# Values as bf16 in 1 KB reads, keys in 2 KB rows, early weights re-timed: an attention and spectral-mix kernel on one core

## Chip, cores, metric

The kernel runs on one core of a Trainium2 chip. The metric is device time in microseconds (us), the median of several executions; lower is better. All runs compared here are fast (within 1.5% of the fastest run of the same kernel).

## The reference

Sliding-window attention with a decay by distance, then a mix of the lowest 64 frequencies over the tokens by complex matrices, then a channel matrix. q, k, v are 8 x 8 x 576 x 64 in f32 (9.4 MB each); the spectral weights are 2 x 64 matrices of 512 x 512 in f32 (134 MB). One of them (the imaginary part of frequency 0) is not needed.

```python
scores = scale * q @ k.T                       # per batch and head, 576 tokens
scores = where(0 <= i - j < 128, scores - slope[h] * (i - j), -1e9)
x = concat_heads(softmax(scores) @ v)          # 8 x 576 x 512
X = rfft(x, axis=1)
Y[:, :64] = X[:, :64] * (w_r + 1j * w_i)       # per frequency a 512 x 512 matrix
u = x + irfft(Y)
out = u + relu(u @ w_ch)
```

## The kernel before

Attention comes first, in 16 units (8 batches x 2 groups of four heads). Work of neighbouring units is interleaved in "stages". The inputs of unit u + 2 are loaded when unit u's are cast to bf16. Meanwhile early spectral weights are fetched and converted to bf16 on the way (issued from GpSimd): one per stage, held back by a tiny "gate" copy that waits for an output of the stage before. After attention the other weights stream in as f32 into memory that attention leaves. Cuts are marked.

```python
# loads: values in pairs of tokens (j=2), so rows of 512 B; keys in nine tokens, rows of 2304 B
            t = self.raw[w][:, u % 2]
            sv = self.v[b, hs]
            for h in range(4):
                nc.sync.dma_start(
                    out=t[:, :2, h],
                    in_=sv[h, : FULL * P].rearrange("(r p j) d -> p r (j d)", r=2, j=2),
                )
            nc.sync.dma_start(
                out=t[64:96, 2],
                in_=sv[:, FULL * P :].rearrange("h (p j) d -> p h (j d)", j=2),
            )
        else:
            # ... queries and keys: one DMA of (j=9) rows

# cast of the values (VectorE)
        if w == "v":
            src = src.rearrange("p s h (j d) -> p s h j d", j=2)
            for half in range(2):
                row = slice(64 * half, 64 * half + 64)
                nc.vector.tensor_copy(
                    self.vb[u % 2][row, :, :, :, W * half : W * half + D], src[row, :2])
            nc.vector.tensor_copy(self.vt[u % 2][64:96, :, :, :D], src[64:96, 2])

# AHEAD: how many early weights at the end of which stage; EARLY: how many buffers they have; LATER: into the input buffers once they are free
    AHEAD = {0: 1, 1: 1, 2: 1, 4: 1, 5: 1, 7: 1, 8: 1, 10: 1, 11: 1, 12: 1, 13: 3, 14: 1}
    LATER = {14: 3, 15: 4}
    EARLY, NWA, NWB, AGAIN = 14, 6, 2, 8
# ...
            if stage in AHEAD:
                if stage:
                    b, g = at.units[stage - 1]
                    nc.gpsimd.tensor_copy(gate[:1, :1], x[:1, b, 0, 256 * g : 256 * g + 1])
                load_w(AHEAD[stage], early, True)
            if stage in LATER:
                load_w(LATER[stage], None, True)
# ... after attention: six f32 buffers in the memory it left
        load_w(NWA, wpool, False)
```

The softmax here doesn't subtract the row's maximum and nothing guards it: scores larger than these inputs give would overflow.

## Time and profile before

| | before |
|---|---|
| time, median of the first 4 runs | 451.56 us |
| DMA full | from about 3 to 411 us of the profiled 450.4 us |
| stage of attention (59 to 112 us) | 6.7 us |
| last early weight issued / first f32 weight issued | 124.4 / 125.9 us |
| first spectral matmul | 134.8 us |

In a table of stretches each row is one stretch of the span: its limits, its length, then the busy us of PE, PE weight loads, DVE, ACT and POOL (GpSimd), each with a count, then the granted clock, the DMA share (1 is all 16 engines busy; overlapping packets push it over 1) and GB/s. The prediction below shows that table. What it does not show are DVE's groups of instructions in steady attention, 59 to 112 us (line, engine, operation, out<-in, shapes, count | busy us, mean ns | idle us before):

```profile
L347 DVE TENSOR_TENSOR x<-av,rec 128x640 bf16<-128x640 f32 x16 | 13.2, 824 | 0.5
L233 DVE CAST vb<-vr 64x1024 bf16<-64x1024 f32 x16 | 10.9, 684 | 0.1
L305 DVE TENSOR_TENSOR att<-att,mask 128x1024 bf16<-128x1024 bf16 x16 | 10.3, 685 | 0.0
...
L235 DVE CAST vt<-vr 32x512 bf16<-32x512 f32 x8 | 3.3, 410 | 0.0
```

Eight units' values cost DVE 10.9 + 3.3 us of its 49.4, 1.8 us a unit.

### The profile page before, as it was taken

The numbers are of one execution on the slowest core, as the hardware profiler recorded it, in microseconds if no ns is written. First come the engines' busy times: TensorE is split into PE (matmuls) and PEld (weight loads), VectorE is DVE, ScalarE is ACT, GpSimd is POOL, SyncE is SP. The second block draws the span as 40 slices with busy tenths as digits, with TensorE's granted clock in tenths as the row PEclk, the third lists the DMA queues.
The fourth block names the chain that finished last, engine by engine and source line by source line (L and its number), as shares of the span: only waits on it lengthen the run. The fifth ranks groups of instructions, "written<-read, shape, count | busy, mean of one in ns | idle before, by whom it ended". The sixth has DMA issues, their size and how long they took to land. (4 is left out here: it accounts for less than half of the span.)

```text
span 450.4 us, 8021 instructions
## 1 busy us (share of the span) xinstructions
PE 362.3 (80%) x3314; PEld 193.1 (43%) x3314; DVE 177.0 (39%) x323; ACT 152.7 (34%) x196; POOL 73.9 (16%) x130
## 2 busy tenths in 40 slices
PE   4789899999968275776674766999999998877994
PEld 3457676777755032221222233544444443332331
DVE  7878699999752011010100132121212212220684
ACT  6859799999820000000000010211122110110772
POOL 8600000011512010200000000000000000054881
PEclk9989899999999659565659799999999999999998
DMA  8999999999999999999999999999999999995597
GB/s 282 310 310 319 302 232 303 321 311 263 212 266 319 316 260 314 326 372 427 418 421 421 423 422 419 420 421 420 421 418 421 421 420 421 420 399 206 197 358 295
DMA packets 53768, 157.03 MB, mean 349 GB/s; under 512 B 5205, under 2 KB 24421, under 8 KB 41317
## 3 DMA queue, kind: packets, MB, share of 16 engines
q1 hardware_dynamic: 47908, 140.56, 81.2%
q0 software_dynamic: 5824, 15.97, 18.1%
q8 instruction: 26, 0.43, 0.4%
q14 instruction: 10, 0.07, 0.0%
HBM read 162.53 MB, written 9.44 MB: 382 GB/s over the span
## 5 line engine op out<-in xcount | busy, mean ns | idle before, releaser
L832 PE MATMUL acc<-w,XC 128*32 128x512 bf16 x456 | 130.3, 451 | 42.5 <-DMA w<-in_moe_w_i_dram 22.1
L832 PEld LDWEIGHTS <-XC 128*32 128x32 bf16 x508 | 59.8, 139 | 127.5 <-issue 94.2
L294 ACT ACTIVATE att<-sc 128x1024 bf16<-128x1024 f32 x64 | 64.0, 1031 | 10.2 <-PE sc L284 10.2
L604 ACT CAST ZW<-zw 128x512 bf16<-128x512 f32 x8 | 4.7, 585 | 162.4 <-PE zw L602 162.4
L576 DVE TENSOR_SCALAR yq<-acc 128x512 bf16<-128x512 f32 x13 | 8.9, 688 | 104.6 <-PE acc L832 104.6
L679 ACT CAST XW<-my 128x512 bf16<-128x512 f32 x36 | 19.3, 589 | 75.4 <-PE my L627 75.4
L617 POOL DMA_DIRECT2D Z<-yq x19 | 9.7, 519 | 214.1 <-issue 207.7
L331 PE MATMUL av<-vb,att 128*128 128x132 bf16 (+1 forms) x576 | 39.0, 219 | 5.7 <-DVE x L347 3.9
L331 PEld LDWEIGHTS <-att 128*128 128x128 bf16 x704 | 37.2, 99 | 11.2 <-DVE x L347 8.2
L651 DVE COPY xT<-tr 128x1024 bf16<-128x1024 bf16 x18 | 12.5, 692 | 69.7 <-PE tr L649 69.7
L670 PE MATMUL my<-wch,xT 128*64 128x512 bf16 x288 | 34.5, 382 | 0.8 <-DVE xT L651 0.8
L256 ACT COPY qkT<-tp 128x1152 bf16<-128x1152 bf16 x30 | 33.5, 1116 | 3.2 <-PE tp L250 2.5
L284 PE MATMUL sc<-qkT 64*64 64x256 bf16 (+2 forms) x640 | 26.0, 271 | 2.1 <-ACT qkT L256 1.2
L347 DVE TENSOR_TENSOR x<-av,rec 128x640 bf16<-128x640 f32 x32 | 26.4, 824 | 1.1
L784 DVE TENSOR_TENSOR o<-yy,r 128x512 f32<-128x512 f32 (+1 forms) x24 | 21.7, 953 | 6.3 <-ACT r L741 4.6
L284 PEld LDWEIGHTS <-qkT 64*64 64x64 bf16 x640 | 15.0, 111 | 20.1 <-issue 17.1
L670 PEld LDWEIGHTS <-xT 128*64 128x64 bf16 x288 | 14.8, 109 | 18.9 <-issue 6.9
L271 PE MATMUL sc<-bias,ident 128*128 128x512 bf16 x64 | 21.4, 420 | 1.4 <-ACT att L294 1.4
L233 DVE CAST vb<-vr 64x1024 bf16<-64x1024 f32 x32 | 22.2, 694 | 0.3
L606 DVE CAST Z<-z 64x512 bf16<-64x512 f32 x16 | 11.0, 689 | 25.0 <-PE z L599 24.9
L741 ACT ACTIVATE r<-mm 128x512 f32<-128x512 f32 (+1 forms) x24 | 18.1, 811 | 7.4 <-PE mm L627 4.2
L305 DVE TENSOR_TENSOR att<-att,mask 128x1024 bf16<-128x1024 bf16 x32 | 20.6, 684 | 0.0
(133 smaller groups left out, 372.7 us busy)
## 6 DMA issues: line engine op xcount, KB each, us to landing
w<-in_moe_w_i_dram SPq DMA_DIRECT2D x52, 1024.0 KB, 18.0
w<-in_moe_w_r_dram SPq DMA_DIRECT2D x45, 1024.0 KB, 17.9
qr<-in_q_dram SPq DMA_DIRECT2D x16, 576.0 KB, 9.4
kr<-in_k_dram SPq DMA_DIRECT2D x16, 576.0 KB, 7.1
vr<-in_v_dram SPq DMA_DIRECT2D x64, 128.0 KB, 6.5
w<-in_moe_w_r_dram POOLq DMA_DIRECT2D x16, 512.0 KB, 17.3
out_dram<-o SPq DMA_DIRECT2D x10, 512.0 KB, 3.8
out_dram<-o SPq DMA_DIRECT2D x16, 256.0 KB, 3.5
```

The source lines that it names most:

```text
L233: nc.vector.tensor_copy(self.vb[u % 2][row, :, :, :, W * half : W * half + D], src[row, :2])
L256: (self.nc.vector.tensor_copy if u < 2 and w == "q" else self.nc.scalar.copy)(dst.rearrange("q h (p j) -> q h p j", j=TPP), tp.rearrange(" ...
L271: nc.tensor.matmul(sc[:, e], lhsT=self.ident, rhs=self.bias[:, hv].rearrange("p j n -> p (j n)"), start=True, stop=False, skip_group_check ...
L284: nc.tensor.matmul(sc[64 * half : 64 * half + 64, e, j * 256 + c0 : j * 256 + c0 + n], lhsT=qkT[row, 1, h, k0 + j : k0 + P : 2], rhs=qkT[r ...
L294: self.nc.scalar.activation(self.att[u % 2][:, kt * 8 * P : (kt + 1) * 8 * P], sc.rearrange("p e n -> p (e n)"), AF.Exp, scale=1.0 / math. ...
L305: nc.vector.tensor_tensor(out=rows, in0=rows, in1=self.table[:, heads], op=ALU.mult)
L331: nc.tensor.matmul(bank[:, qt * W : qt * W + rhs[j].shape[1]], lhsT=att[:, o : o + P], rhs=rhs[j], start=(n == 0 and j == 0), stop=(n == l ...
L347: nc.vector.tensor_tensor(out=self.x[:, b, :, cs].rearrange("p t (h d) -> p h t d", h=2), in0=tiles[:, :, :, :D], in1=rec.unsqueeze(-1).br ...
L670: nc.tensor.matmul(mm[ROWS[half]], lhsT=lhsT, rhs=wch[:, dt], start=(dt == 0), stop=False, skip_group_check=True,)
L679: nc.scalar.copy(XW[:, j, n], mms[n])
L784: nc.vector.tensor_tensor(out=o[:, c], in0=yy[:, c], in1=r[:, c], op=ALU.add)
L832: nc.tensor.matmul(into[32 * (i // 2) : 32 * (i // 2) + 32], lhsT=window[a], rhs=w[a], start=(ri == 0 and a == 0), stop=(ri == (m > 0) and ...
```

## The change

Its intent: read values in rows of 1 KB rather than 512 B, let the DMA convert them, and use the freed memory for one more early weight. Four tokens in a row land in one partition, so eight copies of 32 partitions bring the quarters to where the matmuls want them. Keys follow the same order of tokens. Buffers are laid out by parity of the unit so that slots for f32 weights come free earlier.

```diff
 def load:
         if w == "v":
-            for h in range(4):
-                nc.sync.dma_start(
-                    out=t[:, :2, h],
-                    in_=sv[h, : FULL * P].rearrange("(r p j) d -> p r (j d)", r=2, j=2),
-                )
+            nc.gpsimd.dma_start(                      # out is bf16
+                out=t[0],
+                in_=self.v[b, hs, : FULL * P].rearrange("h (p j) d -> p h (j d)", j=4),
+            )
+            # ... and the last 64 tokens with j=2
+        elif w == "k":
+            # ... rows of eight tokens (2 KB), the last 64 tokens in rows of two (512 B)
 def cast:
-            for half in range(2):
-                row = slice(64 * half, 64 * half + 64)
-                nc.vector.tensor_copy(
-                    self.vb[u % 2][row, :, :, :, W * half : W * half + D], src[row, :2])
+            for n in range(4):
+                c0 = W * (n % 2)
+                for a in range(2):
+                    r = 64 * (n % 2) + 32 * a
+                    nc.vector.tensor_copy(
+                        self.vb[u % 2][r : r + 32, n // 2, :, :, c0 : c0 + D],
+                        rows[32 * n : 32 * n + 32, :, :, a])
 # ... key transposes ten instead of nine, mask windows eight instead of four, layout by parity
-    AHEAD = {0: 1, 1: 1, 2: 1, 4: 1, 5: 1, 7: 1, 8: 1, 10: 1, 11: 1, 12: 1, 13: 3, 14: 1}
-    LATER = {14: 3, 15: 4}
-    EARLY, NWA, NWB, AGAIN = 14, 6, 2, 8
+    AHEAD = {0: 1, 1: 1, 2: 1, 3: 1, 4: 1, 5: 1, 7: 1, 8: 1, 9: 1, 10: 1, 11: 1, 12: 1, 13: 3}
+    LATER = {14: 3, 15: 2}
+    EARLY, NWA, NWB, AGAIN = 15, 6, 2, 8
 # ... start
-        for w, u in (("q", 0), ("k", 0), ("q", 1), ("k", 1), ("v", 0), ("v", 1)):
+        for w, u in (("q", 0), ("k", 0), ("q", 1), ("k", 1)):
             at.load(w, u)
 # ...
         at.distances(pool)
+        at.load("v", 0)
         at.fixtures(0)
         next(table, None)
+        at.load("v", 1)
         at.fixtures(1)
```

More of the change, by code (lines that the diff above doesn't have):

```diff
@@ L121, in __init__ @@
         fix = ctx.enter_context(tc.tile_pool(name="afix", bufs=1))
-        self.table = fix.tile([P, H, 2, 2 * P], BF16, name="mask")
-        self.bias = fix.tile([P, H, 2, 2 * P], BF16, name="bias")
-        self.vb = [fix.tile([P, 2, 4, 2, 2 * W], BF16, name=f"vb{i}") for i in range(2)]
-        self.vt = [fix.tile([P, 4, 2, W], BF16, name=f"vt{i}") for i in range(2)]
-        self.qkT = [fix.tile([P, 2, 2, (FULL + 1) * P], BF16, name=f"qkT{i}") for i in range(2)]
-        self.att = [fix.tile([P, FULL * 8 * P + 64], BF16, name=f"att{i}") for i in range(2)]
+        both = [[], []]
+        for i in range(2):
+            vb = fix.tile([P, 2, 4, 2, 2 * W], BF16, name=f"vb{i}")
+            vt = fix.tile([P, 4, 2, W], BF16, name=f"vt{i}")
+            att = fix.tile([P, FULL * 8 * P + 64], BF16, name=f"att{i}")
+            table = fix.tile([P, 4, 2, 2 * P], BF16, name=f"mask{i}")
+            bias = fix.tile([P, 4, 2, 2 * P], BF16, name=f"bias{i}")
+            qT = fix.tile([P, 2, S], BF16, name=f"qT{i}")
+            kT = fix.tile([P, 2 * S + 32], BF16, name=f"kT{i}")
+            both[i] = vb, vt, att, table, bias, qT, kT
+        self.vb, self.vt, self.att, self.table, self.bias, self.qT, self.kT = zip(*both)
         self.loaded, self.casted, self.open = {}, {}, {}
@@ L145, in distances, with window @@
         key_i = pool.tile([P, 2, 2], I32)
-        for half in range(2):
-            nc.gpsimd.iota(key_i[64 * half : 64 * half + 64], [[1, 2], [-P, 2]], base=0,
-                           channel_multiplier=2)
+        for r in range(4):
+            nc.gpsimd.iota(key_i[32 * r : 32 * r + 32], [[2, 2], [-P, 2]], base=r % 2,
+                           channel_multiplier=4)
+        last_i = pool.tile([P, 2], I32)
+        nc.gpsimd.iota(last_i[64:], [[1, 2]], base=0, channel_multiplier=2)
         key = pool.tile([P, 2, 2], FP32)
         nc.gpsimd.tensor_copy(key, key_i)
+        last = pool.tile([P, 2], FP32)
+        nc.gpsimd.tensor_copy(last[64:], last_i[64:])
         self.near = [pool.tile([P, 2, 2 * P], BF16) for _ in range(2)]
-        def window(out, half, c0, width, n):
-            row = slice(64 * half, 64 * half + 64)
+        def window(out, row, c0, width, n, values, first, j, p):
             sign = 1 - 2 * n
@@ L157, in window @@
                 out=out[row, :, c0 : c0 + width],
-                in_=key[row, :, n].unsqueeze(-1).broadcast_to([64, 2, width]),
-                compare_op=ALU.is_ge, fill=-float(2**20), base=-n,
-                pattern=[[-sign, 2], [sign, width]], channel_multiplier=-2 * sign,
-            )
-        for half in range(2):
+                in_=values.unsqueeze(-1).broadcast_to([row.stop - row.start, 2, width]),
+                compare_op=ALU.is_ge, fill=-float(2**20), base=-n - sign * first,
+                pattern=[[-sign * j, 2], [sign, width]], channel_multiplier=-sign * p,
+            )
+        for r in range(4):
+            row = slice(32 * r, 32 * r + 32)
             for n in range(2):
-                window(self.near[0], half, n * P, P, n)
+                window(self.near[0], row, n * P, P, n, key[row, :, n], r % 2, 2, 4)
         nc.gpsimd.tensor_copy(self.near[1][:64], self.near[0][:64])
         nc.gpsimd.tensor_copy(self.near[1][64:, :, : P + TAIL], self.near[0][64:, :, : P + TAIL])
-        window(self.near[1], 1, P + TAIL, TAIL, 0)
+        window(self.near[1], slice(64, P), P + TAIL, TAIL, 0, last[64:], 0, 1, 2)
     def slope(self, h):
-        return 2.0 ** (-8.0 * (h + 1) / self.table.shape[1])
+        return 2.0 ** (-8.0 * (h + 1) / (4 * self.NG))
     def decay(self, h):
-        self.nc.scalar.activation(self.table[:, h], self.near[0], AF.Exp, scale=self.slope(h))
+        self.nc.scalar.activation(self.table[h // 4][:, h % 4], self.near[0], AF.Exp, scale=self.slope(h))
     def offset(self, h):
-        self.nc.vector.tensor_scalar_mul(self.bias[:, h], self.near[1], math.sqrt(D) * self.slope(h))
+        self.nc.vector.tensor_scalar_mul(self.bias[h // 4][:, h % 4], self.near[1],
+                                         math.sqrt(D) * self.slope(h))
     def inverse_table(self):
@@ L204, in load @@
         if w == "v":
-            t = self.raw[w][:, u % 2]
-            sv = self.v[b, hs]
-            for h in range(4):
-                nc.sync.dma_start(
-                    out=t[:, :2, h],
-                    in_=sv[h, : FULL * P].rearrange("(r p j) d -> p r (j d)", r=2, j=2),
-                )
-            nc.sync.dma_start(
-                out=t[64:96, 2],
-                in_=sv[:, FULL * P :].rearrange("h (p j) d -> p h (j d)", j=2),
-            )
+            t = self.raw["v"][:, u % 2], self.raw["t"][64:96, u % 2]
+            nc.gpsimd.dma_start(
+                out=t[0],
+                in_=self.v[b, hs, : FULL * P].rearrange("h (p j) d -> p h (j d)", j=4),
+            )
+            nc.gpsimd.dma_start(
+                out=t[1],
+                in_=self.v[b, hs, FULL * P :].rearrange("h (p j) d -> p h (j d)", j=2),
+            )
+        elif w == "k":
+            t = self.raw[w][:, u % 2]
+            for e in range(2):
+                src = self.k[b, 4 * g + 2 * e : 4 * g + 2 * e + 2]
+                for row, j0, n, part in ((slice(0, P), 0, 8, src[:, : FULL * P]),
+                                         (slice(0, 64), 8, 2, src[:, FULL * P :])):
+                    nc.sync.dma_start(
+                        out=t[row, e, j0 : j0 + n].rearrange("p j d -> p (j d)"),
+                        in_=part.rearrange("h (p j) d -> p h (j d)", j=n),
+                    )
         else:
             t = self.raw[w][:, u % 2]
-            src = (self.q, self.k)["qk".index(w)][b, hs]
             nc.sync.dma_start(
                 out=t.rearrange("p e j d -> p e (j d)"),
-                in_=src.rearrange("(e h) (p j) d -> (h p) e (j d)", h=2, j=TPP),
+                in_=self.q[b, hs].rearrange("(e h) (p j) d -> (h p) e (j d)", h=2, j=TPP),
             )
@@ L229, in cast @@
         if w == "v":
-            src = src.rearrange("p s h (j d) -> p s h j d", j=2)
-            for half in range(2):
-                row = slice(64 * half, 64 * half + 64)
-                nc.vector.tensor_copy(
-                    self.vb[u % 2][row, :, :, :, W * half : W * half + D], src[row, :2])
-            nc.vector.tensor_copy(self.vt[u % 2][64:96, :, :, :D], src[64:96, 2])
+            rows = src[0].rearrange("p h (j a d) -> p h j a d", j=2, a=2)
+            for n in range(4):
[5 more added lines that the diff above has]
+                        rows[32 * n : 32 * n + 32, :, :, a])
+            nc.vector.tensor_copy(self.vt[u % 2][64:96, :, :, :D],
+                                  src[1].rearrange("p h (j d) -> p h j d", j=2))
         else:
-            dst = self.mid.tile([P, TPP, 2, D], BF16, tag=w, name=w)
+            dst = self.mid.tile([P, src.shape[2], 2, D], BF16, tag=w, name=w)
             nc.vector.tensor_copy(dst.rearrange("p j e d -> p e j d"), src)
@@ L244, in transpose @@
         src = self.casted.pop((u, w))
-        if (u, w) == (0, "k"):
-            tp = self.ps.tile([P, TPP, P], BF16, tag="sc", bufs=2, name="tp")
-        else:
-            tp = self.ps.tile([P, TPP, P], BF16, tag="tp", name="tp")
-        for j in range(TPP):
-            nc.tensor.transpose(tp[:, j], src[:, j].rearrange("p e d -> p (e d)"), self.ident)
-        self.open[w, u] = tp
+        tag = dict(tag="sc", bufs=2) if (u, w) == (0, "k") else dict(tag="tp")
+        tp = self.ps.tile([P, TPP * P], BF16, name="tp", **tag)
+        self.open[w, u] = tp
+        if w == "q":
+            for j in range(TPP):
+                nc.tensor.transpose(tp[:, j * P : (j + 1) * P],
+                                    src[:, j].rearrange("p e d -> p (e d)"), self.ident)
+            return
+        main = tp[:, : FULL * 2 * P].rearrange(
+            "d (h j b a i p) -> d j a i h b p", h=2, j=2, b=FULL, a=2, p=16, i=2)
+        rest = tp[:, FULL * 2 * P :].rearrange("d (j h i p) -> d j h i p", j=2, h=2, i=2)
+        for j in range(8):
+            nc.tensor.transpose(
+                main[:, j // 2 % 2, j % 2, j // 4], src[:, j].rearrange("p e d -> p (e d)"),
+                self.ident.rearrange("k (b p h) -> k h b p", b=FULL, h=2))
+        for j in range(2):
+            nc.tensor.transpose(
+                rest[:, j], src[:64, 8 + j].rearrange("p e d -> p (e d)"),
+                self.ident[:64, :64].rearrange("k (p i h) -> k h i p", i=2, h=2))
     def evacuate(self, u, w):
         tp = self.open.pop((w, u))
-        dst = self.qkT[u % 2][:, "qk".index(w), :, : self.S]
-        (self.nc.vector.tensor_copy if u < 2 and w == "q" else self.nc.scalar.copy)(
-            dst.rearrange("q h (p j) -> q h p j", j=TPP),
-            tp.rearrange("q j (h p) -> q h p j", h=2),
+        if w == "k":
+            self.nc.scalar.copy(
+                self.kT[u % 2][:, : 2 * self.S].rearrange("d (c p i) -> d c p i", p=16, i=2),
+                tp.rearrange("d (c i p) -> d c p i", p=16, i=2))
+            return
+        (self.nc.vector.tensor_copy if u < 2 else self.nc.scalar.copy)(
+            self.qT[u % 2].rearrange("q h (p j) -> q h p j", j=TPP),
+            tp.rearrange("q (j h p) -> q h p j", h=2, p=64),
         )
@@ L263, in score @@
         nc = self.nc
-        qkT = self.qkT[u % 2]
+        qT, kT = self.qT[u % 2], self.kT[u % 2]
         pair, h = t // 2, t % 2
@@ L269, in score @@
             for e in range(2):
-                hv = 4 * self.units[u][1] + 2 * e + h
                 nc.tensor.matmul(
-                    sc[:, e], lhsT=self.ident, rhs=self.bias[:, hv].rearrange("p j n -> p (j n)"),
+                    sc[:, e], lhsT=self.ident, rhs=self.bias[self.units[u][1]][:, 2 * e + h].rearrange("p j n -> p (j n)"),
                     start=True, stop=False, skip_group_check=True,
@@ L277, in score @@
                 blk = 2 * pair + half
-                spans = [(blk * P, 0, min(2 * P, self.S - blk * P))]
+                spans = [(512 * h + 256 * j + 64 * blk, blk * P, 0, min(2 * P, self.S - blk * P))]
                 if blk == FULL - 1:
-                    spans.append((FULL * P, 192, TAIL))
-                for k0, c0, n in spans:
+                    spans.append((FULL * 2 * P + 64 * j + 32 * h, FULL * P, 192, TAIL))
+                for k0, q0, c0, n in spans:
                     for e in range(2):
@@ L285, in score @@
                             sc[64 * half : 64 * half + 64, e, j * 256 + c0 : j * 256 + c0 + n],
-                            lhsT=qkT[row, 1, h, k0 + j : k0 + P : 2],
-                            rhs=qkT[row, 0, h, k0 : k0 + n],
+                            lhsT=kT[row, k0 : k0 + 64], rhs=qT[row, h, q0 : q0 + n],
                             start=not biased, stop=True, skip_group_check=biased,
@@ L303, in mask @@
         rows = att.rearrange("p (e j n) -> p e j n", e=2, j=2)
-        heads = slice(4 * g + t % 2, 4 * g + 4, 2)
-        nc.vector.tensor_tensor(out=rows, in0=rows, in1=self.table[:, heads], op=ALU.mult)
+        nc.vector.tensor_tensor(out=rows, in0=rows, in1=self.table[g][:, t % 2 :: 2], op=ALU.mult)
     def value(self, u, e):
@@ L433 @@
     rawpool = actx1.enter_context(tc.tile_pool(name="raw", bufs=1, side="right"))
-    raw = {w: rawpool.tile([P, 2, 2, TPP, D], FP32, name=w + "r") for w in "qk"}
-    raw["v"] = rawpool.tile([P, 2, 3, 4, 2 * D], FP32, name="vr")
+    raw = {w: rawpool.tile([P, 2, 2, n, D], FP32, name=w + "r") for w, n in (("q", TPP), ("k", 10))}
+    raw["v"] = rawpool.tile([P, 2, 4, 4 * D], BF16, name="vr")
+    raw["t"] = rawpool.tile([P, 2, 4, 2 * D], BF16, name="vtr")
     spare = [raw[w][:, i].rearrange("p e j d -> p (e j d)") for w in "qk" for i in range(2)]
-    vflat = raw["v"].rearrange("p u s h d -> p (u s h d)")
-    spare += [vflat[:, 2 * DM * i :] for i in range(3)]
-    spare = [t[:, : 2 * DM].bitcast(BF16).rearrange("p (a e) -> p a e", a=4) for t in spare]
+    spare = [t[:, : 2 * DM].bitcast(BF16) for t in spare]
+    spare.append(raw["v"].rearrange("p u h d -> p (u h d)"))
+    spare = [t.rearrange("p (a e) -> p a e", a=4) for t in spare]
     wq, homes, todo_w, again = {}, {}, [0, *range(2, 2 * NM)], []
@@ L462 @@
         n = len(at.units)
-        for w, u in (("q", 0), ("k", 0), ("q", 1), ("k", 1), ("v", 0), ("v", 1)):
+        for w, u in (("q", 0), ("k", 0), ("q", 1), ("k", 1)):
             at.load(w, u)
+        nc.vector.memset(raw["k"][64:, :, :, 8:], 0.0)
         done = set()
@@ L480 @@
         nc.vector.memset(norm[:32], 1.0 / S)
-        for t in at.qkT:
-            nc.vector.memset(t[:, 1, :, S:], 0.0)
+        for t in at.kT:
+            nc.vector.memset(t[:, 2 * S :], 0.0)
         at.distances(pool)
+        at.load("v", 0)
         at.fixtures(0)
         next(table, None)
+        at.load("v", 1)
         at.fixtures(1)
```

## The prediction

> **What bounds the kernel now.** I read the page's second part first (40 slices of the span), then the table of stretches, then the groups of instructions, then the DMA issues, then the packet records of the trace counted by size. From the page:
>
> ```profile
> PE   4789899999968275776674766999999998877994
> DVE  7878699999752011010100132121212212220684
> PEclk9989899999999659565659799999999999999998
> DMA  8999999999999999999999999999999999995597
> GB/s 282 310 310 319 302 232 303 321 311 263 212 266 319 316 260 314 326 372 427 418 421 421 423 422 419 420 421 420 421 418 421 421 420 421 420 399 206 197 358 295
> ```
>
> The DMA row is 9 from the second slice to the 36th (about 11 to 405 us), while no engine's row is. The GB/s row says that this full time buys about 420 GB/s in the second half but only some 300 in the first eleven slices, the attention. Part of that gap is only bookkeeping: the weights fetched early are converted from f32 to bf16 on the way, and the row counts the half-size written bytes. Counting source bytes from the packet records (twice the size for converting packets), I get 38.1 MB between 3 and 112 us, 349 GB/s, against 420 GB/s from 130 to 405 us. So attention loses about 109 x (1 - 349/420) = 18 us of DMA time. That is all a better load pattern can fight for. The table of stretches:
>
> ```profile
> 59.00:112.00 53.00, 50.01 (x920) 38.73 (x919) 49.38 (x90) 50.10 (x57) 5.95 (x12) 1.00 1.06 291
> 112.00:130.00 18.00, 15.92 (x293) 12.33 (x293) 12.69 (x25) 13.41 (x15) 7.13 (x13) 1.00 1.03 218
> 130.00:195.00 65.00, 40.53 (x214) 19.11 (x210) 8.71 (x27) 0.55 (x2) 8.89 (x20) 0.74 1.04 311
> 195.00:405.00 210.00, 174.09 (x977) 76.09 (x976) 35.97 (x73) 24.59 (x45) 6.34 (x13) 0.90 1.02 418
> ```
>
> After the stretch's length come busy us of PE, weight loads, DVE, ACT and POOL, then the granted clock, the DMA share and GB/s. In steady attention (59 to 112 us) PE, DVE and ACT are each 93 to 95% busy, so the three nearly tie, and the DMA share is 1.06 as well. From 130 us on only the DMA is full. The matmul group of the spectral stage waits for weights, and the queue's issues are deep:
>
> ```profile
> w<-in_moe_w_i_dram SPq DMA_DIRECT2D x52, 1024.0 KB, 18.0
> qr<-in_q_dram SPq DMA_DIRECT2D x16, 576.0 KB, 9.4
> kr<-in_k_dram SPq DMA_DIRECT2D x16, 576.0 KB, 7.1
> vr<-in_v_dram SPq DMA_DIRECT2D x64, 128.0 KB, 6.5
> ```
>
> A 1 MB weight needs 2.5 us at 420 GB/s and lands 18 us after issue: seven are queued. So until the last weight lands (about 411 us) the time is the sum of DMA work plus DMA idle time; the 39 us behind it (the chain that ended last starts at 416.6 us) are not touched. A faster or slower attention changes nothing by itself, as long as the DMA never runs dry.
>
> **The Trainium skill.** "DMA: Bandwidth & Descriptors", Specifications, puts the smallest transfer for line rate at 512 B. This trace differs: 512 B packets take 27 ns at the median (31 mean), 19 bytes per ns, where 8192 B packets take 313 (26 per ns). So there is something to gain in theory. The same page, "Issuing engines are not separate DMA queues", says all queues share the same 16 engines; the trace agrees (converting weights on the software queue take 0.69 of the engines between 130 and 160 us and the plain ones 0.35, sum 1.04), so moving values to another queue adds no rate. "SBUF - State Buffer", "SBUF: two separate sides", warns that descriptors written by GpSimd wait while DVE runs its two-port modes; here DVE is 93% busy, yet each of GpSimd's weight issues takes only 0.53 us. "VectorE: DVE Perf Modes", "What auto-detection actually checks": 16-bit copies inside SBUF can go twice as fast as f32 ones. The trace agrees: a 512-element bf16 copy takes 285 ns, a 512-element f32 cast 410.
>
> **The change part by part.**
>
> 1. Values, DMA. Removed: 18,432 packets of 512 B (16 units x 1152), mean 31.1 ns, over 16 engines 35.8 us. Added: 16 x 512 packets reading 1 KB and 16 x 128 reading 512 B, all converting. The trace has no such packet. A plain 1 KB packet takes 46 ns at its fastest; converting cost 322 against 313 ns at 8192 B and 96 against 84 at 2048 B (the late channel matrix against the output writes), so I add about 11: estimates 57 and 38 ns. Sum (8192 x 57 + 2048 x 38)/16 = 34 us unloaded, up to 39 us if load inflates it as it did the old ones (31.1/27). So **-2 to +3 us**: the bigger read is paid back by the conversion's fixed cost, since the number of packets only falls from 1152 to 640 and each costs nearly twice as much.
> 2. Keys, DMA. Was 4096 packets of 2304 B, mean 104.7: 26.8 us. Becomes 4096 of 2048 B (84 ns x the same 1.10 = 93) and 2048 of 512 B (31): 27.7 us. **+1 us**.
> 3. Weights. Early slots 14 to 15, two more early weights issued before stage 13 (at stages 3 and 9), late ones in spare buffers 7 to 5: 20 converted before the f32 stream instead of 21. The bytes from HBM are the same. One converting weight becomes plain: 128 x (331 - 316)/16 = 0.1 us. What it can gain is DMA idle time: the stretch from 55 to 60 us has a DMA share of 0.81, the only hole in attention, some 1 to 1.5 us. A weight at stage 3 (near 42 us) and faster refills should fill it: **-1 to -1.5 us**.
> 4. DVE. Per unit it drops 2 x 690 + 410 ns of value casts and gets eight 32-row bf16 copies of 512 elements and a tail, 9 x 0.28 = 2.5 us, +0.7 us; key cast +0.07 (1280 instead of 1152 elements). Overlap of neighbours (about 50 ns each) makes it +0.5. DVE had about 0.45 us of idle time in a 6.7 us stage, so DVE becomes the bound and the stage perhaps 7.0 to 7.2 us.
> 5. PE: ten key transposes for nine (about +0.1 us), contiguous 64-column score weights. ACT: same element counts, 1.12 us per evacuation.
> 6. Start: GpSimd makes eight distance windows instead of four (+2.5 us at 0.63 each) and issues the first values behind them, so the first exponentials come 1 to 2 us later. The queue then holds four 0.59 MB loads (some 6 us), so perhaps 0 to 1 us of DMA idle is added.
>
> Attention thus ends some 4 to 9 us later (it hands over at 134.8 us now), all beside a busy DMA. Inputs plus 20 weights are 28.3 + 21.0 = 49.3 MB, which at 349 GB/s from 3 us keep the DMA busy until 144 us. The reordered memory lets the first f32 slots open when the last even unit is done, before that. So I expect no hole at the handover.
>
> Sum: -2..+3, +1, -1.5, -0.1, 0..+1, centre about +0.5 us. I lean faster than that sum because mixed traffic inflates packets (2304 B: median 95, mean 104.7) and half as many value packets may lower this for queries and keys too: 8192 x 5/16 = 2.5 us. That gives about **450.5 us**.
>
> **Rivals.**
> (a) Bigger reads do remove most of attention's loss. For it: 512 B packets carry 13 of the 18 us of loss ((31.1 - 19.5) x 18,432/16). If a converting 1 KB packet cost only 46 ns loaded, values would take 27 us, 9 less, and with the hole the time would be about 442. Against it: the conversion surcharge.
> (b) DVE becomes the bound and the DMA runs dry at the handover. For it: the 93% and the added 0.5 us a stage, one weight fewer as buffer. Against it: the 10 us of queue above. It would cost 2 to 6 us: 454 to 458.
> (c) Values now stand behind whole weights in one software queue, and descriptors compete with DVE's ports; attention waits for values. For it: weights there land after 17.3 us. Against it: a value load has two stages, 13 us, and a weight ahead of it is 3 to 5 us. Lateness again counts only if the DMA idles; up to +5 us.
> (d) All of it is hidden, 452.
>
> **Range and chances.** 450.5, with (a) pulling to 443 and (b), (c) to 457: range 445 to 456. Faster by over 2% needs 9 us, all of (a): 0.07. Slower by over 2% needs 461, (b) and (c) together: 0.05. Within 2%: 0.88.
>
> **What would show it.** Value packets of 512 B written taking 50 to 65 ns (right) or 46 and less (rival a). DMA share near 1.05 with source rate near 350 GB/s in attention. DVE over 96% busy there, its eight copies at about 0.28 us; if they take 0.4, (b) gains. The first spectral matmul at 138 to 144 us while the DMA row stays 9; a digit below 9 near 130 to 145 us would be (b). The last weight landing 0 to 4 us earlier, with an unchanged tail. The prediction is wrong if the loss in attention came from mixing queues rather than from packet sizes, or if the tail moves.

## The result

The changed kernel takes 457.51 us (455.55 to 458.72, 4 runs) against 451.56 (450.14 to 452.37, 4 runs). The ratio is 1.0131, 95% interval 1.0086 to 1.0176. A ratio here is the mean time of one kernel's fast runs over the mean of the other's of the same rounds, so it is not quite the ratio of the medians quoted. The prediction, 450.5 with a range of 445 to 456, missed on the slow side.

The changed kernel's page, busy tenths in 40 slices of its 455.2 us:

```profile
PE   4578898889896755756766676999999999877993
DVE  6699899999983200010101024121212112220684
PEclk9999999999999977786566699999999999999999
DMA  8989999999899999999999999999999999996597
GB/s 266 203 216 279 274 257 241 245 275 271 125 201 285 316 314 318 326 380 425 421 421 421 422 423 418 421 419 420 422 420 420 420 419 421 420 402 243 194 354 293
```

DVE's digits stay at 8 and 9 two slices longer. The DMA row has an 8 in the third and in the eleventh slice (about 23 to 34 and 114 to 125 us), where it had a 9; GB/s in those slices are 216 and 125, where the kernel before had 310 and 212 (its slices are nearly as long). Part of that fall is bookkeeping, as the values, now converted, count half; the DMA shares below have no such effect. The table of stretches, on the changed kernel, with the same limits as in the prediction and finer ones below:

```profile
59.00:112.00 53.00, 47.67 (x838) 35.74 (x835) 51.22 (x125) 46.08 (x52) 18.53 (x26) 1.00 1.09 257
112.00:130.00 18.00, 16.54 (x287) 12.17 (x286) 16.82 (x41) 15.55 (x18) 8.87 (x14) 1.00 0.93 153
130.00:195.00 65.00, 43.54 (x350) 24.14 (x348) 15.13 (x44) 5.94 (x9) 9.45 (x21) 0.84 1.04 304
195.00:405.00 210.00, 176.11 (x974) 76.35 (x973) 36.66 (x74) 24.60 (x45) 3.89 (x8) 0.89 1.01 419
```

```profile
18.00:23.00 5.00, 0.40 (x12) 0.16 (x4) 4.87 (x8) 2.08 (x4) 4.40 (x8) 1.00 0.77 136
23.00:28.00 5.00, 2.81 (x32) 2.10 (x33) 4.94 (x13) 2.90 (x3) 2.46 (x3) 1.00 0.63 136
120.00:125.00 5.00, 4.71 (x85) 3.29 (x84) 4.49 (x10) 4.49 (x6) 4.38 (x8) 1.00 0.74 88
```

And the same stretches of five us of the kernel before:

```profile
18.00:23.00 5.00, 3.53 (x39) 2.82 (x40) 4.99 (x12) 4.58 (x6) 0.53 (x1) 1.00 1.04 272
23.00:28.00 5.00, 5.00 (x79) 3.51 (x80) 2.54 (x6) 2.96 (x3) 0.68 (x2) 1.00 1.06 353
120.00:125.00 5.00, 4.49 (x89) 3.63 (x86) 4.10 (x8) 3.98 (x6) 3.64 (x7) 1.00 1.06 213
```

The reader is to see two holes of the DMA, one near 18 to 28 us and one at 120 to 125 us, where the DMA share was above 1 before. DVE rose from 49.4 to 51.2 of 53 us, and its stage from 6.7 to 7.4 us (eight stages lie between the gate copies at 62.95 and 122.35 us). DVE's groups between 59 and 112 us in the changed kernel:

```profile
L252 DVE COPY vb<-vr 32x512 bf16<-32x512 bf16 x61 | 17.3, 284 | 0.7
...
L255 DVE COPY vt<-vtr 32x512 bf16<-32x512 bf16 x7 | 2.0, 285 | 0.2
```

The gate of stage 13, and the first weight of the burst behind it, in the kernel before and in the changed one:

```profile
112.48 0.51 POOL L524 COPY gate<-x 1x1 bf16<-1x1 bf16 x1 [5.67 <-DVE x L347]
112.94 0.53 POOL L451 DMA_DIRECT2D w<-in_moe_w_i_dram  x1
```

```profile
122.35 0.51 POOL L562 COPY gate<-x 1x1 bf16<-1x1 bf16 x1 [0.27 <-DVE x L381]
122.81 0.55 POOL L486 DMA_DIRECT2D w<-in_moe_w_i_dram  x1
```

**An account in bytes.** From the packet records I counted the source bytes landed by a given time (converting packets at twice their written size). In the streaming stage the DMA moves 0.42 MB per us, so a deficit divided by 0.42 is a lag in us. The third block is DMA idle time: the missing part of 16 packets in flight, summed.

| | landed by 30 us | 110 us | 125 us | 140 us | idle before 30 | 30 to 110 | 110 to 145 us |
|---|---|---|---|---|---|---|---|
| before | 9.8 MB | 37.5 | 43.1 | 49.4 | 2.4 us | 1.6 | 0.5 |
| changed | 7.5 | 37.0 | 41.2 | 47.2 | 7.0 | 1.8 | 2.9 |

The changed kernel is 5.3 us behind at 30 us (2.24 MB), catches up to 1.4 us at 110 us, falls back to 5.3 us at 140 us, and keeps that lag to the end of the weights: the last f32 weight packet ends at 415.9 us instead of 411.3. What follows then takes 39.3 us instead of 39.1. So the loss is made before 140 us, and the middle of attention looks **better** than before: 29.4 MB instead of 27.8 between 30 and 110 us.

### The profile page after: what moved, and what is told of

It is laid out like the page before. It is cut to its first block, busy times and chain, and to the rows that moved or that the text cites. A ratio compares the mean times of both kernels' runs of the same rounds, so it can differ in the third digit from the quotient of the medians.

```text
span 455.2 us, 8161 instructions
## 1 busy us (share of the span) xinstructions
PE 364.7 (80%) x3330; PEld 192.4 (42%) x3330; DVE 192.1 (42%) x420; ACT 152.9 (34%) x196; POOL 103.2 (23%) x170
## 5 line engine op out<-in xcount | busy, mean ns | idle before, releaser
L870 PE MATMUL acc<-w,XC 128*32 128x512 bf16 x464 | 134.7, 445 | 47.8 <-DMA w<-in_moe_w_r_dram 29.0
L252 DVE COPY vb<-vr 32x512 bf16<-32x512 bf16 x128 | 39.0, 305 | 3.7 <-DMA vr<-in_v_dram 2.2
L216 POOL DMA_DIRECT2D vr<-in_v_dram x16 | 18.2, 1140 | 59.4 <-DVE vb L252 59.4
L320 PE MATMUL sc<-qT,kT 64*64 64x256 bf16 (+2 forms) x640 | 25.5, 267 | 2.6 <-ACT kT L289 2.0
L320 PEld LDWEIGHTS <-kT 64*64 64x64 bf16 x640 | 14.7, 110 | 19.6 <-issue 16.0
```

Of the source, the lines that this page charges most:

```text
L216: nc.gpsimd.dma_start(out=t[0], in_=self.v[b, hs, : FULL * P].rearrange("h (p j) d -> p h (j d)", j=4),)
L252: nc.vector.tensor_copy(self.vb[u % 2][r : r + 32, n // 2, :, :, c0 : c0 + D], rows[32 * n : 32 * n + 32, :, :, a])
L320: nc.tensor.matmul(sc[64 * half : 64 * half + 64, e, j * 256 + c0 : j * 256 + c0 + n], lhsT=kT[row, k0 : k0 + 64], rhs=qT[row, h, q0 : q0 ...
L870: nc.tensor.matmul(into[32 * (i // 2) : 32 * (i // 2) + 32], lhsT=window[a], rhs=w[a], start=(ri == 0 and a == 0), stop=(ri == (m > 0) and ...
```

## The experiments

Theory H: the time is lost in holes, in which nothing is issued to the DMA. Loads and early weights are issued stage by stage, and the stage got longer through DVE. Rivals: P, the new packets cost more DMA time; S, the late start alone is to blame. Kernels ran beside the kernel before, whose median was 451.73 us (e1 to e4), 449.57 (e5 to e8), 450.31 (e9 to e11) and 449.58 (e12; one run of the kernel before took 1591 us, that the ratios leave out). Compare ratios, not times. The trace of the kernel before that is used throughout is not of these: e6 is level with it by the ratio (1.0002), yet its profiled span is 2.0 us shorter (448.4 against 450.4). So the leads over that trace given for e8, e10 and e12 may be about 2 us too large.

| run | median us | ratio to before | 95% interval |
|---|---|---|---|
| changed | 457.51 | 1.0131 | 1.0086 to 1.0176 |
| e1_start | 457.64 | 1.0132 | 1.0106 to 1.0159 |
| e2_burst | 452.88 | 1.0036 | 1.0009 to 1.0064 |
| e3_start_burst | 454.32 | 1.0067 | 1.0038 to 1.0096 |
| e4_half_copies (wrong result) | 450.89 | 0.9987 | 0.9959 to 1.0016 |
| e5_before_dve | 455.58 | 1.0129 | 1.0093 to 1.0165 |
| e6_spread | 449.86 | 1.0002 | 0.9973 to 1.0031 |
| e7_before_vpool | 455.52 | 1.0134 | 1.0100 to 1.0168 |
| e8_pool_copies | 448.77 | 0.9978 | 0.9952 to 1.0005 |
| e9_cast512 | 448.32 | 0.9944 | 0.9913 to 0.9975 |
| e10_start_pool4 | 451.27 | 1.0001 | 0.9970 to 1.0032 |
| e11_start_pool2 | 450.90 | 1.0001 | 0.9969 to 1.0032 |
| e12_before_spread | 454.18 | 1.0090 | 1.0042 to 1.0138 |

### e1_start: fill the first hole

```diff
         at.load("v", 1)
+        load_w(2, early, True)
         at.fixtures(1)
-    AHEAD = {0: 1, 1: 1, 2: 1, ...
+    AHEAD = {2: 1, ...
```

> The changed kernel, with its first two early weights issued right after the values of unit 1 (near 17 us) instead of at the ends of stages 0 and 1 (24.8 and 32.6 us); nothing else moves. Theory H (holes: the DMA has nothing issued from 18 to 28 us and again from 120 to 125 us): the first hole closes (DMA share 18 to 28 us from 0.77 and 0.63 to about 1), but the number of early weights before the last burst at the end of stage 13 is the same, so what is gained at the start is lost again as a longer second hole near 120 us. Time 457 +-1.5. Rival P (the converting packets and the 512 B key tails simply cost more engine time, 38.1 against 35.8 us and 28.7 against 26.8 us by their records): also about 457, but with no hole near 120 us longer than before. Rival S (the start hole alone cost the 5 us): 452 to 453.

Measured: 457.64 us, nothing gained. The first hole did close (DMA share 1.08 and 1.04 from 18 to 28 us, lag at 30 us down to 0.8 us). From 120 to 125 us the share was 0.73, and the lag at 125 us 4.3 us (4.6 in the changed kernel). Rival S falls: by 115 us the lags behind the kernel before were 0.6 us (changed) and 0.3 (e1): both kernels had worked off nearly all that was issued, and a better start was waited away. Between 30 and 110 us e1 landed 27.8 MB, no more than the kernel before.

### e2_burst: fill the second hole

```diff
-    ... 11: 1, 12: 1, 13: 3}
+    ... 11: 1, 12: 4}
```

> The changed kernel with the three weights of the end of stage 13 issued at the end of stage 12 (near 115 us instead of 123 us); nothing else moves. Theory H: the second hole (DMA share 0.74 from 120 to 125 us) closes and 3 to 4.5 us come back: 453 to 454.5. Rival P: no hole matters, 457. Rival S: 457.

Measured: 452.88 us, by the ratios some 4.3 us less than the changed kernel. The second hole is gone:

```profile
120.00:125.00 5.00, 4.89 (x88) 3.81 (x88) 4.50 (x11) 4.49 (x5) 3.26 (x6) 1.00 1.06 211
```

The packets are the same, so P does not explain the loss. Nearly three quarters of it was this one hole: queries and keys were all loaded at about 116 us, only the last unit's values (0.6 MB of f32) were still to be issued, at 120.4 us, and the last burst of weights stood behind the gate of stage 13 until 122.8 us (112.9 us before the change).

### e3_start_burst: both

The edit is that of the two runs above together.

> Both moves of weights together. Theory H: both holes are filled, and as source bytes flow somewhat faster in the middle of attention than in the kernel before (368 against 346 GB/s between 30 and 115 us), the kernel comes out 7 to 9 us faster than the changed one: 448.5 to 451, at or just under the kernel before (451.6). Rival P: 457. Rival S: 452 to 453.

Measured: 454.32 us, a miss of theory H by 3 us or more. Its lag at 30 us was 0.9 us, yet 0.5 at 115 us and 1.6 at 140 us. What the start gains is still lost between 30 and 110 us, where DMA idle time and slack come with one weight a stage or none. A hole can only be turned into time if later stages issue more as well.

### e4_half_copies: less DVE work (wrong result)

```diff
-                for a in range(2):
+                for a in range(2 if u < 2 else 1):
```

> Wrong result on purpose: from unit 2 on, four of the eight quarter copies of the values are left out, 4 x 0.28 = 1.1 us of DVE less a unit, DMA and its schedule untouched. Theory H with DVE as the cause of the second hole: stage length falls from 7.4 to about 6.7 us, the last burst comes near 113 us, the attention ends 8 to 10 us earlier, the second hole closes and 3 to 4 us come back: 453 to 454; the start hole stays. Rival P: 457, as attention's length does not matter to a full DMA.

Measured: 450.89 us, better than expected, and level with the kernel before, though neither the loads nor the schedule were touched. The stage fell to 7.0 us, the last burst came at 116.6 us, and between 30 and 110 us 30.2 MB landed. So DVE's copies are a cause: they pace every issue, not only the end of attention.

### e5_before_dve: the same DVE burden on the kernel before

```diff
             nc.vector.tensor_copy(self.vt[u % 2][64:96, :, :, :D], src[64:96, 2])
+            for _ in range(3):
+                nc.vector.tensor_copy(self.idle[:32, 1], self.idle[:32, 0])   # 32 x 512 bf16, unused
```

> The kernel before with three idle 32-row bf16 copies of 512 elements (0.28 us each) added to DVE after each unit's value casts, loads and schedule untouched. Theory H2 (a longer DVE stage alone makes the DMA run dry, because loads and early weights are issued stage by stage): stage from 6.7 to about 7.4 us, the last bursts of weights come 8 to 10 us later, a DMA hole appears between about 112 and 125 us, time 454.5 to 457. Rival D (attention's length is hidden behind a full DMA, as the prediction had it): 451.5 to 452.5, DMA share 1.0 throughout.

Measured: 455.58 us, ratio 1.0129, as large as the whole loss of the change (the two need not add up: the change also has its start hole on one side and its cheaper inputs on the other). The copies took 282 ns, the stage became 7.2 us, and a hole opened some ten us before the place of the second one of the changed kernel (the last burst came at 116.3 us here):

```profile
110.00:115.00 5.00, 4.12 (x79) 3.51 (x79) 4.78 (x13) 4.32 (x6) 0.00 (x0) 1.00 0.80 157
115.00:120.00 5.00, 4.61 (x85) 3.59 (x82) 4.61 (x9) 4.70 (x6) 2.04 (x4) 1.00 0.83 161
```

Rival D of that run, and with it the prediction's main premise, falls: 0.85 us more DVE work per unit (3 x 282 ns; the change adds 2.56 - 1.79 = 0.77) is not hidden behind the DMA.

### e6_spread: the same weights, issued evenly and earlier

```diff
-    AHEAD = {0: 1, 1: 1, 2: 1, 3: 1, 4: 1, 5: 1, 7: 1, 8: 1, 9: 1, 10: 1, 11: 1, 12: 1, 13: 3}
+    AHEAD = {0: 1, 1: 1, 2: 1, 3: 1, 4: 1, 5: 1, 6: 1, 7: 1, 8: 1, 9: 1, 10: 1, 11: 2, 12: 2}
```

> The changed kernel with the same fifteen early weights issued by the end of stage 12, but spread: one also at stage 6, two at stages 11 and 12, none at 13. Theory H: the DMA is starved of issues wherever a stage has no weight; against the version with three moved to stage 12 (452.9) the hole near 75 us and the slack of the middle are filled too: 450.5 to 452. Rival P or no slack left in the middle: 452.5 to 454, and values landing later behind weights.

Measured: 449.86 us, ratio 1.0002: the schedule alone takes back the whole loss, with DVE as busy as in the changed kernel (51.2 of 53 us). DMA idle time falls to 0.5 us between 30 and 110 us and to 0.1 from there to 145 us:

```profile
59.00:112.00 53.00, 46.51 (x832) 35.45 (x838) 51.19 (x125) 45.88 (x52) 20.29 (x30) 1.00 1.12 264
120.00:125.00 5.00, 4.89 (x87) 3.81 (x87) 4.50 (x11) 4.49 (x5) 3.30 (x6) 1.00 1.18 206
```

### e7_before_vpool: values on the other queue, unconverted

```diff
-                nc.sync.dma_start(out=t[:, :2, h], ...      # values of the kernel before, f32
+                nc.gpsimd.dma_start(out=t[:, :2, h], ...
```

> The kernel before with the values still as f32 in 512 B packets but issued from GpSimd, so on the other queue, as in the changed kernel. It tells why the busy DMA moved 368 GB/s of source bytes between 30 and 115 us in the changed kernel against 346 before. If two queues overlapping each other's packets is the reason: some 365 GB/s here while busy too (mean packets in flight above 18). If the larger reads are: about 346. Time itself is not the point (GpSimd has ten issues a stage; later start): 451 to 457.

This run asks why the middle looks better. I took the busy DMA time between 30 and 110 us (16 packets in flight counting as full), subtracted 2.5 us per MB-sized weight (at the streaming rate), and divided by the MB of inputs: 3.02 us per MB in the kernel before, 2.80 in the changed one, 2.77 in e6, and about 3.0 here. So moving the values to the other queue alone did not make inputs cheaper. But the packets did not stay the same, as was intended: the 18,432 value packets of 512 B became 2304 records of 4096 B (178 ns at the median).

The count also moves with the schedule. With the loads of the changed kernel it is 2.93 in e1 and 2.94 in e3, where 8.0 weights landed in the stretch, against 2.77 in e6 and 2.74 in e8 with 10.3 and 10.7. With the loads of the kernel before it is 3.04 in e5 with 8.0 and 2.90 in e12 with 10.9. So about half of the fall from 3.02 goes with the number of weights, and the loads are only to be compared at a like number. The time (455.52) is no answer by itself: with the values issued from GpSimd the DMA share was 0.88 from 18 to 23 us and 0.73 from 115 to 120 us.

### e8_pool_copies: half of the copies on GpSimd (right result)

```diff
-                    nc.vector.tensor_copy(
+                    (nc.gpsimd if u > 1 and a else nc.vector).tensor_copy(
 # with the AHEAD of e6_spread
```

> The spread weights of the other run of this call, and from unit 2 on four of the eight quarter copies on GpSimd instead of DVE (right result). GpSimd is 35% busy in attention and a 64-row copy took it 0.6 us, so 4 x 0.6 = 2.4 us fit in its stage. Theory H: DVE falls by 1.1 us a unit as in the run with half the copies (450.9, stage 6.9 us), the second hole is closed by the schedule as well, so 448 to 450. Rival: GpSimd and DVE block each other and DVE's instructions get longer, stage stays near 7.4 us: 452.

Measured: 448.77 us, ratio 0.9978; the interval just touches 1. The rival had a part in it, for the copies that stayed on DVE took longer:

```profile
L252 DVE COPY vb<-vr 32x512 bf16<-32x512 bf16 x30 | 13.5, 452 | 0.3
```

452 ns instead of 284, so of the 1.1 us a unit that left DVE some 0.7 came back (4 x 0.17), and the stage was 7.1 us.

### e9_cast512: conversion without the larger reads

```diff
-    raw["v"] = rawpool.tile([P, 2, 3, 4, 2 * D], FP32, name="vr")
+    raw["v"] = rawpool.tile([P, 2, 3, 4, 2 * D], BF16, name="vr")
-                nc.sync.dma_start(out=t[:, :2, h], ...      # 512 B rows as in the kernel before
+                nc.gpsimd.dma_start(out=t[:, :2, h], ...
 # layout, keys, masks and the two 64-row casts as in the kernel before;
 # EARLY 15 and AHEAD as in e6_spread, LATER {14: 3, 15: 2}, start of the values as in the change
```

> The kernel before with its values still read in 512 B pieces (two tokens) but converted to bf16 on the way from GpSimd, keys as before, no quarter copies: three DVE copies of bf16 a unit (two of 64 rows x 1024, about 0.4 us each, and the tail 0.28 = 1.1 us, against 1.79 before and 2.6 in the changed kernel). Freed memory goes to a fifteenth early slot, early weights in the spread schedule. It parts the two halves of 'bf16 in 1 KB reads'. Counting weights at 2.5 us each, the busy DMA spent 3.02 us per MB of inputs between 30 and 110 us in the kernel before, 2.99 with the values on GpSimd's queue unconverted, 2.75 to 2.81 with the change. If the 1 KB reads are what helps: 3.0 or more here (pieces written are only 256 B). If the conversion helps by itself: about 2.8. Time: DVE at 6.2 us a stage, so no longer stage than before; 447 to 452, the better the cheaper the conversion.

Measured: 448.32 us, ratio 0.9944 (0.9913 to 0.9975), the only version clearly under the kernel before. Inputs cost 2.83 us per MB. At a like number of weights that stands between 2.90 (e12, neither conversion nor larger rows) and 2.77 and 2.74 (e6 and e8, both); over the stretch from 40 to 110 us the same four are 2.80, 2.90, 2.80 and 2.75. So conversion without 1 KB reads brings a part of the gain, from not quite half to all of it; the count is too coarse to say more. And without quarter copies DVE is relieved instead of loaded:

```profile
59.00:112.00 53.00, 48.12 (x865) 37.31 (x865) 41.51 (x83) 46.66 (x52) 31.37 (x50) 0.97 1.22 264
112.00:130.00 18.00, 16.92 (x301) 12.96 (x302) 13.09 (x27) 16.10 (x20) 9.37 (x16) 1.00 1.20 202
```

DVE is busy 41.5 of 53 us (49.4 before, 51.2 changed), and the DMA has no idle time after 40 us. The value casts are now 64x1024 bf16 copies of 422 ns (684 from f32).

### e10_start_pool4 and e11_start_pool2: all repairs together

The edits are those of e1, e6 and e8; e11 puts two of the eight copies on GpSimd (`a and n > 1`) instead of four.

> The changed kernel with all three repairs: two early weights at the start, the rest spread to stage 12, and four of eight quarter copies on GpSimd from unit 2 on. Theory H: with the middle of attention full, the 2.5 to 3.5 us that the start hole costs are no longer lost later, so 1 to 2.5 us faster than without the start weights (0.9978 of before): ratio 0.992 to 0.997. Rival: values and queries of the first units come later behind the two weights and attention shifts: 0.998 to 1.0.

> As the run with all three repairs, but only two quarter copies on GpSimd. With four there, the copies left on DVE took 452 ns instead of 284[...]. If that blocking grows with the number on GpSimd, two save DVE about as much (0.5 us a unit) as four, and the ratio is within 0.002 of the other.

Measured: 1.0001 both. e10 misses its expectation, and its own rival's figure fits. In its profile the start did pay up to 120 us (5.4 us ahead of the kernel before, 4.5 in e8), but everything issued was done by then, and the weights into the input buffers were not issued before 122.5 us: the DMA share was 0.88 from 120 to 125 us (in e8 they came at 123.0, and the share was 0.95). Its profiled execution (span 447.0) does not show why the timed runs were slower than e8's by 0.2%; that stays open. e11 has the same ratio as e10, as expected: with two copies on GpSimd those on DVE took 293 ns, with four 470, so DVE was spared about 0.5 us a unit by two and 0.4 by four. That this is why the times are equal is not shown.

### e12_before_spread: the even schedule on the kernel before

```diff
-    AHEAD = {0: 1, 1: 1, 2: 1, 4: 1, 5: 1, 7: 1, 8: 1, 10: 1, 11: 1, 12: 1, 13: 3, 14: 1}
+    AHEAD = {0: 1, 1: 1, 2: 1, 3: 1, 4: 1, 5: 1, 6: 1, 7: 1, 8: 1, 9: 1, 10: 1, 11: 1, 12: 2}
```

> The kernel before, with only its fourteen early weights moved forward to one per stage and two at stage 12, as in the repaired kernels. It tells how much of the 0.9944 of the 512 B converting version is the schedule. If the schedule alone does it: 0.993 to 0.996. If the DMA of the kernel before has no slack to fill (busy share 0.98 between 30 and 110 us, 2 us of idle), at most 0.5 us: 0.998 to 1.0, and weights earlier only make inputs land later.

Measured: 454.18 us, ratio 1.0090, worse than either expectation. So e9's gain is not the schedule alone. The trace shows the opposite failure: the bytes landed ran 3.7 us ahead by 110 us, the inputs came late (DVE waited 7.9 us for queries and 5.1 us for values between 20 and 130 us; in the kernel before 2.4 us for queries, and values are not among the waits listed), attention ended later, the first f32 weight was issued at 140.1 us instead of 125.9, and the DMA, all early slots filled, ran dry:

```profile
130.00:135.00 5.00, 4.31 (x62) 3.71 (x63) 2.70 (x5) 1.70 (x2) 0.00 (x0) 0.66 0.99 227
135.00:140.00 5.00, 3.87 (x74) 2.92 (x72) 3.88 (x7) 3.04 (x5) 1.05 (x2) 1.00 0.16 20
```

I read it so: with inputs at 2.8 us per MB (e6) such a schedule fits, and with the dearer inputs of the kernel before (2.90 in this run) it does not. No run varies that cost alone, so this is not shown. Nor does any run part the conversion in e9 from the DVE time that it saves.

## Why the prediction was wrong, point by point

- **What bounds the kernel.** "A faster or slower attention changes nothing by itself, as long as the DMA never runs dry" was true as worded, and the step that failed is the next one, "So I expect no hole at the handover" (from "keep the DMA busy until 144 us"). I divided all prefetchable bytes by a rate and forgot that bytes count only once they are issued. Weights are issued by stage number; a longer stage moved the last burst from 113 to 123 us, while all queries and keys had landed by 116 us. So the DMA share was 0.74 from 120 to 125 us (1.06 before), and 2.9 us of DMA time stood idle from 110 to 145 us (0.5 before). e5 shows that the stage alone costs 1.29%, e2 and e6 that issuing earlier gives most (1.0036) or all (1.0002) of it back.
- **Rival (b)** named this outcome (454 to 458) and came true; I weighed it too lightly. Its site was only nearly right: the hole lay before the last burst, not after it.
- **Part 4, DVE:** the copies took 284 ns as said; the stage became 7.4 us, not 7.0 to 7.2, and DVE 96.6% busy. The first spectral matmul came at 144.3 us, 9.5 us later ("4 to 9"). Right in kind, somewhat small. The agreement claimed with the VectorE page is one of direction: 410 to 285 ns is a factor of 1.44, not two.
- **Part 6, start:** "perhaps 0 to 1 us of DMA idle" was 4.5 us (7.0 against 2.4 before 30 us). The first values were issued at 10.0 us, their first eight copies took 5.0 us instead of 2.4 beside GpSimd's fills, and the next query cast stood behind them. Other executions of the same start had 5.0 to 5.8 us (e2, e4). Yet e1 shows that this hole costs nothing as long as later stages have slack.
- **Part 1, packets of values:** 60 ns (64 mean) and 41 ns; "50 to 65" held, and the sum of records is 38.1 us, inside my "34 to 39". But as DMA time it was misleading: the records sum to more than before (35.8 us), yet more packets are in flight at once (17.8 against 16.9 between 30 and 110 us), and the inputs became cheaper by 0.22 us per MB; at a like number of weights it is 0.10 to 0.16, over the 28.3 MB some 3 to 4.5 us if it held throughout. So a part of the gain sought by rival (a) exists; e9 shows that some of it comes with the conversion alone. The added "lean" of 2.5 us for less inflation was in the right direction. Taken whole it would have given 449.6 (451.6 + 0.5 - 2.5); the 450.5 takes only some 1.6 of it, and does not say why.
- **Part 2, keys:** 2048 B rows and 512 B tails could not be told apart from the rest. No run isolates them.
- **Part 3, weights:** two more before stage 13 and none at 14 did not fill the holes, as the extra ones came at stages 3 and 9.
- **Rival (c):** values landed 7.8 us after issue, well within two stages; no wait of DVE for them beyond 2.2 us at the start. It did not happen.
- **The tail** stayed: 39.3 against 39.1 us.
- **A reading:** 0.69 and 0.35 of the engines for the two queues are, on the clock of the views, of 119.5 to 149.5 us. From 130 to 160 us I count 0.53 and 0.50; the sum is 1.04 in both.

## What to carry to other kernels

A full DMA hides compute only where transfers are already issued: if issues are tied to stages of compute, a longer stage shifts every later issue, so work out when each transfer is issued, not only how many bytes are left. Do not add up packet durations as DMA time when packets overlap; compare bytes landed by time. Judge a load pattern by what it makes the busiest engine do afterwards: the plain conversion (e9) brought a part of the DMA gain and took work off DVE (41.5 of 53 us), where the 1 KB rows brought eight copies a unit (51.2). And before two loads are compared by a rate, see what the rate does when only the schedule moves.

## What the Trainium skill lacked or had wrong

- "DMA: Bandwidth & Descriptors", Specifications, gives 512 B as enough for line rate: here 512 B packets took 27 ns at the median (19 bytes per ns, against 26 at 8192 B), and inputs made of 2304 and 512 B packets cost 3.02 us per MB where large weights cost about 2.4 (1/0.42). That the size of the packets alone is the reason is not shown: in e7 the values' records were of 4096 B, and the cost was still about 3.0.
- The same page has no figure for what conversion costs: records of converting packets were 41 ns (256 B written), 60 (512), 96 (1024) and 322 (4096). Yet with values converted at 512 B read and 256 B written (e9) the inputs were not dearer (2.83 us per MB, against 2.90 in e12), with 19.6 packets in flight on average between 30 and 110 us on 16 engines. By how much a sum of packet records overstates DMA time is on no page that I read.
- "SBUF — State Buffer", "SBUF: two separate sides", says that GpSimd and DVE lock each other out of a port pair that they share. It has no figure for such small copies side by side: DVE's copies of 284 ns took 293 ns with two copies a unit on GpSimd (e11) and 452 to 470 ns with four (e8, e10). No run shows that this lock is the cause.
